# Attention and two expert layers in one kernel: the plan of the order gets other numbers for transfers, and the slots of the work between the matmuls are set again

## The chip, the core and the metric

The kernel runs on one core of one Trainium2 chip. The metric is device time in microseconds (us) of one execution; the kernel before was timed in three runs. TensorE is called PE, its weight loads PEld, VectorE DVE, ScalarE ACT, GpSimd POOL, SyncE SP.

## The reference

```python
# attention: 8 batches x 8 heads x 576 rows x 64; keys and values pooled by 8 to 72
k_p = k.reshape(B, H, 72, 8, D).mean(axis=3)
v_p = v.reshape(B, H, 72, 8, D).mean(axis=3)
scores = matmul(q, k_p^T) / sqrt(D)
attn = exp(scores - max); attn = attn / (sum(attn) + 1e-09)
x = matmul(attn, v_p)                       # becomes 4608 tokens x 512
# first layer, 512 -> 2048 -> 512
h = x @ moe_w_in;  x = maximum(0.01 * h, h) @ moe_w_out
# second layer, 512 -> 2048 -> 512
h = x @ moe2_w_in; out = (h * clip(h + 3, 0, 6) / 6) @ moe2_w_out
```

## The kernel before

**The work.** All matmuls of the two layers keep fp32 accuracy: each operand is split into a high and a low part (fp32r), and three products are added. The attention is cut into 24 units (three for each of the 8 batches). A unit has a load of its queries (tile `q`, one buffer, so the next unit's queries can be fetched only when the scores of the unit before have read it), loads of keys and values (tile `raw`, two buffers), sums over 8 on DVE, scores on PE (L492), a maximum on DVE (L508), exps on ACT (L517), a reciprocal, two normalizations on DVE (L535, L548), transposes on PE (L594, L574), copies of them on ACT, and the values' matmuls on PE (L626). The first layer goes over tiles of 512 tokens: for 16 blocks `f` of 128 hidden units a `gemm1` (12 matmuls, L752 to L754) into a bank `h`, the leaky relu on ACT (L767) and DVE, and a `gemm2` (12 matmuls, L801 to L803). The weights of that layer come in a packed form, 1 MB for each `f`, and are decoded by ACT (L666, L668) and DVE (L671, L679, L322). The first tile uses only the first 8 blocks, and its other half is done later. Later tiles of the first layer go in pairs with 7 products in place of 8 (`Pair1`), and the whole second layer does so too (`Pair`); their left factors are written to DRAM (`left1`, `left2`) and read back.

**What sets the order.** No order is written out by hand. Each piece of work is a task with an engine, a cost in ns and the tasks that it needs. `Plan.place` lays the tasks out in time: one free time for each engine, one of them for all DMAs together; a task that needs another starts no sooner than that one's end plus a lag from a table `LAG` (with `plan.landing` on top behind a DMA). `Plan.order` does this 12 times, forward and back, keeps the shortest result, and issues all instructions in the order of their planned starts; each engine then goes through its own instructions strictly in that order. A DMA costs its bytes divided by a rate, plus a constant. Up to the first `gemm2`, a gap of PE in the plan is filled with small matmuls on zeros (`idle<-zeros`, L1615), one for each 56 ns of the gap beyond 200 ns.

**Which tasks stand where before the plan.** PE's tasks keep the order in which the program lists them. A list of steps (`gemm1`, `gemm2` of one `f`) has numbered slots, and the table `C` says in which slot the scores, transposes, values of a unit, the decoding of a weight block or the making of a left factor are listed: `when0` for the weights in the first tile, `att0` for units 2 to 5 there, `quick` and `slow` for the distances between scores, transposes, the third transpose, values and the next unit's sums; `when1`, `att1`, `att2` and so on for later tiles. `flex` is the number of tasks for which a copy may go to ACT or DVE, whichever the plan finds free.

**Transfers.** All DMAs are issued by SP in one order. A load into a tile is issued when the readers of that tile's former content are done; whatever stands behind it on SP waits as well. A write waits for the instruction that makes its data.

Of the kernel before, what the change touches and what calls it, by code (L numbers as in the profile page):

```python
# [30 lines left out]
C = dict(  # L31
    n32=1,
    soon={0: 2000, 1: 4000, 2: 6000},
    flex=536,
    mid=8,
    half0=3,
    steps0='rffrfffr',
    when0=[0, 0, 0, 4, 3, 5, 13],
    att0=[0, 9, 27, 30],
    sec0=4,  # L40
    half1=0,
    steps1='ffffffffffffffff',
    when1=[9, 14, 15, 19],
    att1=[32, 41],
    sec1=23,
    att2=[7],
    quick=[0, 1, 0, 2, 5],
    slow=[0, 4, 5, 5, 4],
    left1=[[(0, 41), (1, 10)], [(2, 4), (3, 3)]],
    att3=[0, 5, 8, 10, 20, 36],  # L50
    gaps3=[0, 2, 2, 2, 0],
    prep3=[17, 48],
    att5=[11, 19, 33, 44, 54, 62],
    gaps5=[0, 3, 2, 9, 4],
    prep5=[94, 156],
    att7=[0, 19, 35],
    gaps7=[1, 12, 11, 13, 18],
    prep7=[87, 97],
    left2=[[(0, 10)], [(1, 16)], [(2, 22)], [(3, 55), (4, 22), (5, 50)], [(6, 18), (7, 51)]],
)  # L60
SCORES = 1700
EXPS = 1782
TRANSPOSES = 260
FIRST_LOADS = 1.25
WARM_FROM = 2700
ENGINES = ("pe", "act", "dve", "gp", "dma")
FIRST = {"dma": 1700.0, "gp": 600.0, "dve": 700.0}


def _f32(bits):  # L70
# [3 lines left out]
class Buf:  # L74


    def __init__(self, plan, pool, tag, shape, dtype, bufs):
        row = plan.tags.setdefault(tag, [])
        self.prev = row[-bufs] if len(row) >= bufs else None
        if self.prev is not None:  # L80
            self.prev.gone = True
        self.gone = False
        row.append(self)
        self.args = (pool, tag, shape, dtype, bufs)
        self.name = f"{tag}_{len(row)}"
        self.tile = None
        self.users, self.writers, self.readers = set(), {}, {}
# [24 lines left out]
class Plan:  # L112
# [8 lines left out]
        ("dve", "dve"): 125,  # L121
        ("act", "act"): 0,
        ("pe", "pe"): 0,
        ("dma", "dma"): 2150,
    }

    def __init__(self):
        self.tags, self.tasks, self.fill_until, self.sooner = {}, [], None, {}
        self.extra, self.landing = [], 0

    def add(self, engine, cost, emit, reads=(), writes=(), other=None):

        n = len(self.tasks)
        after = set()
        over = lambda d, key: (t for k, v in d.items() if all(a == b for a, b in zip(k, key)) for t in v)
        for v in (*reads, *writes):
            assert not v.buf.gone, v.buf.name
            if v.buf.prev is not None:
                after |= v.buf.prev.users
        for v in reads:  # L140
            before = {t for key in v.keys for t in over(v.buf.writers, key)}
            assert before, v.buf.name
            after |= before
        for v in writes:
            for key in v.keys:
                after.update(over(v.buf.writers, key))
                after.update(over(v.buf.readers, key))
        after.discard(n)
        for v in reads:
            for key in v.keys:  # L150
                v.buf.readers.setdefault(key, set()).add(n)
            v.buf.users.add(n)
        for v in writes:
            for key in v.keys:
                v.buf.writers.setdefault(key, set()).add(n)
            v.buf.users.add(n)
        self.tasks.append(([(engine, cost, emit)] + ([other] if other else []), after))
        self.extra.append(self.landing if engine == "dma" else 0)

    def lag(self, a, b):  # L160

        return self.LAG.get((a, b), 1500 if a == "dma" else 1250 if b == "dma" else 180)

    def place(self, ways, after, then, rank, lag, first, back=False):


# [16 lines left out]
        while done < n:  # L183
            best = None
            for e in ENGINES:
                while waiting[e] and waiting[e][0][0] <= free[e]:
                    _, i, k = heapq.heappop(waiting[e])
                    heapq.heappush(ready[e], (rank[i], i, k))
                while ready[e] and way[ready[e][0][1]] is not None:
                    heapq.heappop(ready[e])  # L190
                while waiting[e] and way[waiting[e][0][1]] is not None:
                    heapq.heappop(waiting[e])
                start = free[e] if ready[e] else waiting[e][0][0] if waiting[e] else None
                if start is not None and (best is None or start < best[0]):
                    best = (start, e)
            start, e = best
            free[e] = start
            if not ready[e]:
                continue
            _, i, k = heapq.heappop(ready[e])  # L200
            starts[i], way[i] = start, k
            free[e] = stop = start + ways[i][k][1]
            end = max(end, stop)
            done += 1
            for j in then[i]:
                left[j] -= 1
                late = self.extra[j if back else i]
                for m, w in enumerate(ways[j]):
                    since[j][m] = max(since[j][m], stop + lag(e, w[0]) + late)
                if not left[j]:  # L210
                    offer(j)
        return starts, way, end

    def order(self):
# [19 lines left out]
        for _ in range(ROUNDS):  # L234
            starts, way, end = self.place(ways, after, then, rank, self.lag, FIRST)
            chosen = [w[k] for w, k in zip(ways, way)]
# [20 lines left out]
def attention_moe_moe(ctx: ExitStack, tc: tile.TileContext, qt, kt, vm, vr, wt, wq, eye, mask, out):  # L257
# [15 lines left out]
    plan = Plan()  # L273
    add = plan.add
# [26 lines left out]
        add("pe", n, emit, reads, writes)  # L301

    def on_dma(nbytes, emit, reads, writes):
        add("dma", nbytes / 340 + 60, emit, reads, writes)

    def other(*way):
        return way if len(plan.tasks) < C["flex"] else None
# [19 lines left out]
    def load(dst, src, nbytes):  # L327

        on_dma(nbytes * (FIRST_LOADS if len(plan.tasks) < 60 else 1), lambda: DMA.dma_start(out=dst.ap(), in_=src), [], [dst])

# [317 lines left out]
    left1 = []  # L648
# [4 lines left out]
    def load_w(f, raw):  # L653
        on_dma(
            1 << 20, lambda: DMA.dma_start(out=raw.get().bitcast(I32), in_=wt[ORDER[f]].bitcast(I32)), [], [raw()]
        )
# [29 lines left out]
    def decode_w(f, raw, t, l):  # L686

        decode(raw, t, l)
        wf = buf(f"w{f}", [128, 4, 512], F32R)
        w[f] = wf  # L690
        hi = wf("hi", lambda t: t[:, 0:2].rearrange("p a n -> p (a n)"))
        lo = wf("lo", lambda t: t[:, 2:4].rearrange("p a n -> p (a n)"))
        copy(hi, t, 1024)
        subtract(lo, t, hi, 1024)
        d = chunk[f]()
        on_dma(1 << 19, lambda: DMA.dma_start(out=d.ap(), in_=t.ap()), [t], [d])
        keep(f, wf)
# [222 lines left out]
    left2 = Left(2)  # L920
# [489 lines left out]
    for u in units[:3]:  # L1410
        g = u.n % 2
        a = a13 if g else a12
# [11 lines left out]
    load(mask_sb, mask, 1536)  # L1424
    fetch(u1)
    add("dve", 70, lambda: DVE.memset(three.ap(), 3.0), [], [three])
    room = {0: 8, 1: 9, 2: 10, 3: 14, 4: 15, 5: 14, 6: 15, 7: 14}
    temps = {}

    def weights(f):  # L1430
# [152 lines left out]
    pairs = [Pair(2 * sum(widths[:i]), n) for i, n in enumerate(widths)]  # L1583
# [20 lines left out]
        for k in range(2):  # L1604
            p.jobs.at(56 + 8 * (3 + 2 * k), lambda nxt=nxt, k=k: nxt.prepare(k))
    for p in [*pairs1, *pairs]:
        plan.landing = 250 if p in pairs else 1300
        if p in pairs:
            p.new_spare()
        p.first()  # L1610
        p.second(p is pairs[-1])
# [66 lines left out]
```

## Time and profile before

| what | value |
|---|---|
| time, median of three runs (lowest to highest) | 1571.47 us (1571.19 to 1572.18) |
| the profiled execution: its time | 1572.92 us |
| the profiled execution: span of the instructions | 1571.1 us |
| PE busy | 1564.6 us, 100% of the span |
| DVE busy | 1157.2 us, 74% |
| ACT busy | 969.7 us, 62% |
| granted clock of PE, mean | 1.00 |
| DMA, mean over the span | 259 GB/s |

The profiled execution took 1.45 us more than the median of the three runs, and 1.8 us lie outside the span of its instructions. A busy PE is one that has instructions in work, the small matmuls on zeros among them; it says nothing on whether that work is needed. The rows on which the prediction rests stand in a section below.

### The profile page before, as it was taken

Reading aid. Unit: us, or ns where it says so; the run is one execution under the profiler, and the core shown is the slowest. Engines: PE = TensorE matmul, PEld = TensorE weight load, DVE = VectorE, ACT = ScalarE, POOL = GpSimd, SP = SyncE. Lnnn points to the kernel's source line nnn. Section 1 sums busy time; section 2 is a strip of 40 time slices with the busy share of each in tenths; the row PEclk is TensorE's granted clock in tenths of the full one; section 3 lists DMA queues with packets and bytes.
Section 4 is the critical chain, followed back from the end, with each engine's and each line's share of the span. In section 5 each row is a group of like instructions: output and inputs, shape, how many; then the busy total and the mean of one; then the engine's idle time right before and its main releaser. Section 6 shows DMA issues by size and latency. Waiting matters only on the chain.

```text
span 1571.1 us, 22819 instructions
## 1 busy us (share of the span) xinstructions
PE 1564.6 (100%) x7971; PEld 1342.9 (85%) x7971; DVE 1157.2 (74%) x2000; ACT 969.7 (62%) x2219; POOL 1.9 (0%) x11
## 2 busy tenths in 40 slices
PE   9999999999999999999999999999999999999999
PEld 8888888888888888888888888898899888889988
DVE  7998568568789776985696579559756856875494
ACT  7886476667877677666655455446545544654454
POOL 0000000000000000000000000000000000000000
PEclk9999999999999999999999999999999999999999
DMA  8899778668896898979976567756866675676564
GB/s 313 298 338 313 256 246 272 211 240 285 286 309 225 294 340 298 325 266 335 320 271 224 200 228 248 254 210 218 291 213 230 236 254 210 228 245 229 210 231 143
DMA packets 128322, 406.32 MB, mean 259 GB/s; under 512 B 18512, under 2 KB 47312, under 8 KB 106448
## 3 DMA queue, kind: packets, MB, share of 16 engines
q1 hardware_dynamic: 128208, 404.87, 74.5%
q8 instruction: 63, 1.03, 0.3%
q14 instruction: 51, 0.42, 0.1%
HBM read 317.79 MB, written 87.03 MB: 258 GB/s over the span
## 4 chain that ended last, share of the span: by engine, by line
PE 95%; DVE 3%; ACT 1%; DMA 1%; issue 0%; SPq 0%; DVEq 0%
PE y L1056 37%; PE h L1056 21%; PE a L1056 12%; PE h L752 3%; PE y L801 3%; PE y L802 3%; PE y L803 3%; PE h L754 3%; PE h L753 3%; PE a L626 2%; PE a L492 2%; DVE w L923 1%; PE a L574 1%; PE idle L1615 1%; PE a L594 1%; DVE gl L1251 0%
## 5 line engine op out<-in xcount | busy, mean ns | idle before, releaser
L923 DVE TENSOR_TENSOR w<-y,w 128x512 f32<-128x512 f32 (+2 forms) x108 | 71.0, 658 | 117.5 <-PE y L1056 115.8
L315 ACT ACTIVATE gh<-w 128x460 fp32r<-128x460 f32 (+1 forms) x140 | 82.2, 589 | 65.2 <-PE y L1056 24.8
L923 DVE TENSOR_TENSOR w<-w 128x460 f32<-128x460 f32 (+2 forms) x168 | 104.9, 645 | 3.4 <-ACT w L767 3.0
L1251 DVE SCALAR_TENSOR_TENSOR gl<-w,gh 128x460 fp32r<-128x460 f32 (+1 forms) x140 | 88.4, 633 | 23.5 <-ACT gh L315 23.2
L1056 PE MATMUL y<-w,xh 128*128 128x512 f32 (+2 forms) x444 | 103.9, 383 | 0.0
L1056 PEld LDWEIGHTS y<-w,xh 128*128 128x128 f32 x444 | 82.6, 188 | 13.0
L312 ACT CAST gh<-w 128x512 fp32r<-128x512 f32 x96 | 59.6, 623 | 41.4 <-PE y L1056 21.5
L1222 ACT ACTIVATE gh<-w,three 128x460 f32<-128x460 f32 (+1 forms) x60 | 40.9, 682 | 71.0 <-DVE w L923 71.0
L1056 PE MATMUL y<-w,raw 128*128 128x460 f32 (+1 forms) x384 | 83.4, 370 | 0.0
L801 PE MATMUL y<-gh,w 128*128 128x512 f32 (+2 forms) x204 | 80.3, 394 | 0.1
L752 PE MATMUL h<-xh,w 128*128 128x512 f32 (+2 forms) x204 | 79.8, 391 | 0.0
L1056 PEld LDWEIGHTS y<-w,raw 128*128 128x128 f32 x384 | 72.1, 188 | 8.2
L802 PE MATMUL y<-gl,w 128*128 128x512 f32 (+2 forms) x204 | 78.3, 384 | 0.0
L803 PE MATMUL y<-gh,w 128*128 128x512 f32 (+2 forms) x204 | 78.2, 383 | 0.0
L753 PE MATMUL h<-xl,w 128*128 128x512 f32 (+2 forms) x204 | 77.9, 382 | 0.0
L754 PE MATMUL h<-xh,w 128*128 128x512 f32 (+2 forms) x204 | 77.9, 382 | 0.0
L1056 PE MATMUL y<-w,xl 128*128 128x512 f32 (+2 forms) x324 | 76.8, 385 | 0.0
L322 DVE TENSOR_TENSOR gl<-w,gh 128x512 fp32r<-128x512 f32 x96 | 65.6, 684 | 12.4 <-ACT gh L312 12.4
L322 DVE TENSOR_TENSOR st<-raw,st 128x512 fp32r<-128x512 f32 x88 | 59.7, 685 | 14.7 <-ACT st L312 14.6
L1056 PE MATMUL y<-gh,raw 128*128 128x462 f32 (+1 forms) x224 | 70.0, 373 | 0.0
L517 ACT ACTIVATE s<-a,mx 128x72 f32<-128x72 f32 x204 | 62.5, 345 | 11.7 <-DVE mx L508 11.7
L1056 PEld LDWEIGHTS y<-w,xl 128*128 128x128 f32 x324 | 60.4, 188 | 10.4
(267 smaller groups left out, 4145.0 us busy)
## 6 DMA issues: line engine op xcount, KB each, us to landing
raw<-left SPq DMA_DIRECT2D x68, 1024.0 KB, 4.8
left<-st SPq DMA_DIRECT2D x176, 256.0 KB, 4.7
xh<-left SPq DMA_DIRECT2D x37, 1024.0 KB, 4.8
xl<-left SPq DMA_DIRECT2D x68, 512.0 KB, 5.1
xh<-left SPq DMA_DIRECT2D x56, 512.0 KB, 5.3
w<-left SPq DMA_DIRECT2D x56, 512.0 KB, 5.2
xl<-left SPq DMA_DIRECT2D x25, 1024.0 KB, 4.9
w<-wt SPq DMA_DIRECT2D x16, 1024.0 KB, 8.2
```

The source lines that it names most:

```text
L315: a = lambda: ACT.mul(out=dst.ap(), in_=src.ap(), mul=scale)
L322: lambda: DVE.tensor_tensor(out=dst.ap(), in0=a.ap(), in1=f32(b.ap()), op=ALU.subtract),
L517: ACT.activation(out=at()[:, c, h, :], in_=s4()[:, c, pi, :], func=AF.Exp, bias=mx.get()[:, c, h : h + 1], accum_out=sm.get()[:, 4 * c + h ...
L752: PE.matmul(out=o, lhsT=hi, rhs=xh.get()[:, k, c0:c1], start=k == 0, stop=False)
L753: PE.matmul(out=o, lhsT=hi, rhs=xl.get()[:, k, c0:c1], start=False, stop=False)
L754: PE.matmul(out=o, lhsT=lo, rhs=xh.get()[:, k, c0:c1], start=False, stop=k == 3)
L801: PE.matmul(out=y[:, n0:n1], lhsT=hi, rhs=gh.get()[:, n0:n1], start=start, stop=False)
L802: PE.matmul(out=y[:, c0:c1], lhsT=hi, rhs=gl.get()[:, c0:c1], start=False, stop=False)
L803: PE.matmul(out=y[:, c0:c1], lhsT=lo, rhs=gh.get()[:, c0:c1], start=False, stop=stop)
L923: on_dve(n, lambda: DVE.tensor_tensor(out=dst.ap(), in0=a.ap(), in1=b.ap(), op=op), [a, b], [dst])
L1056: PE.matmul(out=o, lhsT=l, rhs=r, start=first and i == m == 0, stop=last and i == len(left) - 1 and m == 2, skip_group_check=True,)
L1251: lambda: DVE.scalar_tensor_tensor(out=lo.ap(), in0=v.ap(), scalar=1.0 / 6.0, in1=f32(hi.ap()), op0=ALU.mult, op1=ALU.subtract),
```

## The change

The computation stays as it is, and the instructions are the same but for 30 fewer matmuls on zeros (173 in place of 203) and a few copies that go to another engine. What changes is numbers of two kinds. The plan's reckoning of a DMA: up to the end of the tiles that go one by one it takes bytes / 420 + 40 ns (before bytes / 340 + 60) and a lag of 2100 ns to the reader (before 1500), for `Pair1` a rate of 340 and 900 ns on top of the lag (before 1300), for `Pair` a rate of 400 and nothing on top (before 250); the first loads are no longer stretched by 1.25, and DMA is free from 800 ns on (before 1700). And the slots in `C` are others.

```diff
-    flex=536,
+    flex=540,
-    when0=[0, 0, 0, 4, 3, 5, 13],
-    att0=[0, 9, 27, 30],
+    when0=[0, 0, 5, 3, 10, 6, 12],
+    att0=[0, 9, 26, 28],
-    when1=[9, 14, 15, 19],
-    att1=[32, 41],
-    sec1=23,
+    when1=[8, 15, 21, 23],
+    att1=[36, 57],
+    sec1=37,
-    quick=[0, 1, 0, 2, 5],
+    quick=[0, 2, 1, 2, 8],
...
-FIRST_LOADS = 1.25
+FIRST_LOADS = 1.0
-FIRST = {"dma": 1700.0, "gp": 600.0, "dve": 700.0}
+FIRST = {"dma": 800.0, "gp": 600.0, "dve": 700.0}
...
-        ("dma", "dma"): 2150,
+        ("dma", "dma"): 2500,
...
-        self.extra, self.landing = [], 0
+        self.extra, self.landing, self.rate = [], 0, 420
...
-        return self.LAG.get((a, b), 1500 if a == "dma" else 1250 if b == "dma" else 180)
+        return self.LAG.get((a, b), 2100 if a == "dma" else 1250 if b == "dma" else 180)
...
-        add("dma", nbytes / 340 + 60, emit, reads, writes)
+        add("dma", nbytes / plan.rate + 40, emit, reads, writes)
...
-        plan.landing = 250 if p in pairs else 1300
+        plan.landing, plan.rate = (0, 400) if p in pairs else (900, 340)
```

Three places of the order follow. In the rows a name like `w8_2_543` is the second use of buffer `w8`; the last number counts tiles.

DVE, in the first 20 us, from the sum over the keys of unit 1 (`w15_1`, in two halves) and the maxima of unit 0 (`mx_1`, from the scores in `a_1`, `a_2`) on; before:

```order
L389 TENSOR_REDUCE w15_1_95<-w15_1_95 128x72
L508 TENSOR_REDUCE mx_1_189<-a_1_172 128x6
L389 TENSOR_REDUCE w15_1_95<-w15_1_95 128x72
L508 TENSOR_REDUCE mx_1_189<-a_2_174 128x6
L316 TENSOR_SCALAR keys1_1_191<-w15_1_95 128x72
L508 TENSOR_REDUCE mx_2_275<-y2_1_244 128x6
L528 TENSOR_SCALAR inv_1_277<-sm_1_197 128x12
L508 TENSOR_REDUCE mx_2_275<-y3_1_246 128x6
```

and in the changed kernel:

```order
L389 TENSOR_REDUCE w15_1_91<-w15_1_91 128x72 x2
L508 TENSOR_REDUCE mx_1_169<-a_1_146 128x6
L508 TENSOR_REDUCE mx_1_169<-a_2_148 128x6
L508 TENSOR_REDUCE mx_2_220<-y2_1_186 128x6
L508 TENSOR_REDUCE mx_2_220<-y3_1_188 128x6
L457 TENSOR_TENSOR raw_2_162<-h_1_211,mask_1_172 96x256
L313 CAST vrm0_1_247<-raw_2_162 96x256
L528 TENSOR_SCALAR inv_1_249<-sm_1_202 128x12
```

The second half of unit 1's keys is now summed ahead of the first maximum and no longer between the two, and the sums of unit 0's values (`raw_2`, `vrm0`) stand ahead of `inv_1`, with which the normalization of unit 0 begins. On PE 45 matmuls on zeros stand ahead of unit 0's scores in place of 73, 10 between the scores of units 0 and 1 in place of 35, and 47 ahead of the first `gemm1` in place of 35.

ACT, between the first `gemm1` and the copies of the transposes of unit 2 (`a_16`, `a_17` into `w12_1`, which the values' matmuls of unit 2 read); before:

```order
L312 CAST tr_3_678<-a_15_663 96x384
L312 COPY w12_1_70<-a_16_668 128x384
L668 ACTIVATE w13_1_74<-w15_2_603 128x1024
L312 COPY w12_1_70<-a_17_689 128x384
L312 CAST vbd00_1_78<-raw_4_597 64x2x64
L315 ACTIVATE x32_1_383<-a_18_693 128x2x128
L312 CAST xh_1_385<-x32_1_383 128x128 x2
L666 ACTIVATE w12_1_70<-w15_2_603 128x1024
```

and in the changed kernel:

```order
L666 ACTIVATE w12_1_70<-w10_1_299 128x1024
L767 ACTIVATE u_1_564<-h_3_524 128x384
L312 CAST gh_1_78<-u_1_564 128x384
L312 CAST rem_3_573<-rn_3_567 128x3x32 x2
L666 ACTIVATE w11_1_344<-w14_2_351 128x1024
L312 CAST tr_3_590<-a_15_586 96x384
L668 ACTIVATE st_1_593<-w8_2_543 128x512
L312 COPY w12_1_70<-a_16_602 128x384
L312 COPY w12_1_70<-a_17_608 128x384
```

A piece of the decoding of `w8_2` (L668, into `st_1`), one of the weights for the second tile, now stands ahead of the two copies. On PE the transposes and values of unit 2 have moved as well: they stand behind the second `gemm1` (`h_4`) and ahead of the first `gemm2` (L801), with 7, 7 and 6 matmuls on zeros between them; before, 14 of these and then the first `gemm2` and the third `gemm1` stood there, and the transposes and values came after.

SP, around the load of the queries of unit 4 (`q_4`); before, with the loads of `w8_2`, `w9_2` and `w10_2` behind it:

```order
L887 DMA xr_1_977<-spill_1_705 512x1x64
L329 DMA raw_7_982<-kt 128x1152
L329 DMA q_4_1009<-qt 128x768
L655 DMA w8_2_1015<-wt 128x2048
L655 DMA w9_2_1045<-wt 128x2048
L329 DMA q_5_1096<-qt 128x768
L655 DMA w10_2_1108<-wt 128x2048
```

In the changed kernel `w8_2` and `w9_2` stand 20 and 19 rows ahead of `q_4`,

```order
L329 DMA raw_4_472<-vr 96x512
L329 DMA raw_4_472<-vm 128x1024
L655 DMA w8_2_543<-wt 128x2048
L655 DMA w9_2_570<-wt 128x2048
L329 DMA raw_5_606<-kt 128x1152
L655 DMA w14_3_630<-wt 128x2048
L696 DMA chunk2_1_669<-w12_1_70 128x1024
```

and right ahead of it stand another load of 1 MB and two writes of left factors:

```order
L329 DMA raw_7_887<-kt 128x1152
L655 DMA w15_4_908<-wt 128x2048
L696 DMA chunk5_1_949<-w11_1_344 128x1024
L713 DMA left1_10_1_957<-w0_1_387 128x2x256
L713 DMA left1_10_1_957<-w2_1_627 128x2x256
L329 DMA q_4_971<-qt 128x768
```

`w10_2` is one of the rows between the two pieces. Summed over SP's rows, the transfers up to and with `q_4` carry 20,480 KB in the kernel before and 25,088 KB in the changed one; those up to and with `w8_2` carry 12,609 KB in the changed one.

## Rows read from the trace of the kernel before

**Rows 1.** The page, span and section 1 (busy us, share of the span, instructions).

```profile
span 1571.1 us, 22819 instructions
PE 1564.6 (100%) x7971; PEld 1342.9 (85%) x7971; DVE 1157.2 (74%) x2000; ACT 969.7 (62%) x2219; POOL 1.9 (0%) x11
```

**Rows 2.** The chain that ended last, 0 to 60 us, in order: start, us, what.

```profile
0.99 6.91 PE idle L1615 x73
7.90 1.54 PE a L492 x24
...
10.06 3.74 ACT s L517 x24
...
30.56 2.06 PE idle L1615 x35
32.62 0.23 PE h L752
36.88 0.81 PE idle L1615 x14
37.83 0.47 PE y L801
```

**Rows 3.** Stretches of 40 us: busy us of each engine, granted clock, DMA share, GB/s.

```profile
0.00:40.00 40.00, 38.03 (x413) 34.85 (x414) 30.92 (x60) 29.40 (x104) 1.91 (x11) 1.00 0.87 310
...
80.00:120.00 40.00, 40.00 (x223) 33.92 (x222) 38.43 (x71) 33.26 (x81) 0.00 (x0) 1.00 0.96 343
120.00:160.00 40.00, 40.00 (x175) 32.48 (x174) 35.12 (x58) 26.98 (x56) 0.00 (x0) 1.00 0.91 304
400.00:440.00 40.00, 39.52 (x231) 32.68 (x230) 31.66 (x56) 31.87 (x102) 0.00 (x0) 1.00 0.91 321
1360.00:1400.00 40.00, 39.42 (x187) 34.56 (x186) 35.88 (x66) 22.83 (x42) 0.00 (x0) 1.00 0.71 245
```

**Rows 4.** Timeline of DVE, 7 to 11 us: start, us, instruction, idle before.

```profile
7.70 0.75 DVE L389 TENSOR_REDUCE w<-w 128x72 f32<-128x576 f32 x1 [2.17 <-DMA w<-kt]
9.42 0.61 DVE L508 TENSOR_REDUCE mx<-a 128x6 f32<-128x432 f32 x1 [0.97 <-PE a L492]
9.95 0.74 DVE L389 TENSOR_REDUCE w<-w 128x72 f32<-128x576 f32 x1
```

**Rows 5.** Timeline of DVE, 33 to 40 us.

```profile
33.59 1.21 DVE L322 TENSOR_TENSOR w<-w,w 128x1024 fp32r<-128x1024 f32 x1
...
35.93 1.34 DVE L389 TENSOR_REDUCE raw<-raw 128x144 f32<-128x1152 f32 x1
...
39.20 0.95 DVE L548 TENSOR_TENSOR s<-s,inv 128x768 f32<-128x768 f32 x1
```

**Rows 6.** Timeline of ACT, 30 to 43 us.

```profile
30.62 1.14 ACT L666 ACTIVATE w<-w 128x1024 f32<-128x1024 f32 x1
31.66 0.31 ACT L517 ACTIVATE s<-a,mx 128x72 f32<-128x72 f32 x1
...
35.22 0.56 ACT L767 ACTIVATE u<-h 128x384 f32<-128x384 f32 x1
...
42.76 0.49 ACT L312 COPY w<-a 128x384 f32<-128x384 f32 x1
```

**Rows 7.** Timeline of PE, the transposes of unit 2.

```profile
42.05 0.49 PE L574 MATMUL a<-ident,s 128*128 128x128 f32 x3
```

**Rows 8.** DMA, 0 to 75 us: GB/s in 40 slices of 1.875 us, and the total.

```profile
GB/s 11 306 237 342 345 340 417 284 346 415 415 290 15 212 289 434 389 305 414 387 385 112 350 411 66 44 267 249 411 418 419 387 371 278 326 325 341 431 424 149
DMA packets 6133, 23.16 MB, mean 309 GB/s; under 512 B 1263, under 2 KB 1391, under 8 KB 4719
```

**Rows 9.** Issue of q_4 on SP.

```profile
66.06 0.33 SPq L329 DMA_DIRECT2D q<-qt  x1
```

**Rows 10.** Instructions of tile q, 45 to 75 us: its three loads, landing times.

```profile
DMA to landing us min/median/max: 3.4/5.1/8.8
```

**Rows 11.** Timeline of PE, 70 to 74 us: the scores that read q_4.

```profile
73.04 1.11 PE L492 MATMUL a<-keys,q 64*128 64x72 f32 x16
```

More of the change, by code (lines that the diff above doesn't have):

```diff
@@ L42 @@
     steps1='ffffffffffffffff',
-    when1=[9, 14, 15, 19],
-    att1=[32, 41],
-    sec1=23,
-    att2=[7],
-    quick=[0, 1, 0, 2, 5],
[L48 to L52, printed above, removed]
-    att5=[11, 19, 33, 44, 54, 62],
[L54 to L59, printed above, removed]
+    when1=[8, 15, 21, 23],
+    att1=[36, 57],
+    sec1=37,
+    att2=[9],
+    quick=[0, 2, 1, 2, 8],
+    slow=[0, 4, 5, 5, 8],
+    left1=[[(0, 60), (1, 7)], [(2, 7), (3, 7)]],
+    att3=[0, 4, 8, 10, 22, 37],
+    gaps3=[0, 0, 1, 2, 0],
+    prep3=[22, 57],
+    att5=[11, 19, 33, 44, 54, 62],
+    gaps5=[0, 4, 1, 9, 1],
+    prep5=[99, 163],
+    att7=[0, 17, 35],
+    gaps7=[1, 11, 12, 12, 2],
+    prep7=[80, 80],
+    left2=[[(0, 10)], [(1, 22)], [(2, 17)], [(3, 60), (4, 21), (5, 45)], [(6, 15), (7, 56)]],
 )
@@ L1426, in attention_moe_moe @@
     add("dve", 70, lambda: DVE.memset(three.ap(), 3.0), [], [three])
-    room = {0: 8, 1: 9, 2: 10, 3: 14, 4: 15, 5: 14, 6: 15, 7: 14}
+    room = {0: 8, 1: 9, 2: 10, 3: 14, 4: 15, 5: 14, 6: 15, 7: 14, 8: 15, 9: 14}
     temps = {}
```

## Prediction

> **What bounds the kernel now.** I read the page's busy times first: PE works in 1564.6 of 1571.1 us [rows 1], so the kernel is a chain of matmuls and only 6.5 us of the span have no matmul at all. More time hides in matmuls on zeros, and the chain of the first 60 us shows where: 73 of them ahead of unit 0's scores (6.91 us), 35 ahead of the first `gemm1` (2.06 us), 14 between the second `gemm1` and the first `gemm2` (0.95 us from 36.88 to 37.83) [rows 2]. The stretches say the same from the other side: PE is full from 80 to 160 us and misses 0.48 us at 400 to 440 and 0.58 us at 1360 to 1400 [rows 3]. A change of order can therefore win a few us at the start and about 1.1 us later; it can lose wherever PE comes to wait for something that it doesn't wait for now. The second limit in the first 160 us is DMA: its engines are 0.87 to 0.96 busy there, and the most that a stretch of 40 us moved is 343 GB/s, at a share of 0.96 [rows 3]. The plan before reckoned with 340, so its order asked for about what the transfers give. The plan now reckons with 420 in this part.
>
> **The change, part by part.** The sum goes against the profiled execution, 1572.92 us; the median of the runs is 1.45 us less.
>
> *The start.* With 45 matmuls on zeros in place of 73, unit 0's scores can begin about 1 us sooner than at 7.90. But the first maximum on DVE now stands behind both sums over unit 1's keys. The first of these waited for its load until 7.70, and one takes 0.74 to 0.75 us [rows 4]: two in a row end at about 9.2, where the maximum began at 9.42 before. So the exps come 0.2 to 0.3 us sooner than at 10.06 [rows 2], not 1 us. Behind them the sums of unit 0's values stand ahead of `inv_1`, two instructions of some 0.35 us each by my estimate (a 1024-element pass takes 1.21 [rows 5], and these have 256 elements and a fixed part), which gives it back. The other uncertainty is the clock. The first 73 matmuls on zeros took 95 ns each, the 35 later ones 59 ns [rows 2]; so most of the first ran at 1.2 GHz and the later ones at 2.4. With fewer of them the scores (1.54 us) may run at the lower level, up to 1.5 us more. I take **+0.2, from -0.3 to +1.5**.
>
> *Unit 2 and the first `gemm2`.* In the new order PE does the transposes and values of unit 2 between the second `gemm1` and the first `gemm2`. That work is only moved; what costs is the waiting inside it. I follow ACT and DVE from the first `gemm1`, left at 32.6 [rows 2]. Before, three subtractions stood ahead of unit 2's maxima; now they stand behind, so that the 12 exps (3.56 us from 31.66 to 35.22 [rows 6]) end at about 34.7. DVE then has the sum over unit 3's keys (1.27), `inv_3`, a short sum of unit 3's values (half of the former, some 0.6), the reciprocal, `rn_3`, a decoding pass of 1024 (1.14 from start to start) and the rest of the weights, and brings the third transpose's source at about 37.4 [rows 5]. ACT has in that time a decoding pass (1.04 from start to start), the relu and its cast, the casts of the weights' rest, another decoding pass, the copy `tr_3`, and is at 38.6 [rows 6]. There stands the new row, L668 of `w8_2`: half of a pass, 0.5. Then the two copies, 0.37 each (0.49 less the overlap), and PE's values can start at 39.9. PE has been through with `h_4` since 36.9 [rows 2]; of the 3.0 us between, 0.8 is transposes (three of 0.49 less overlap [rows 7]). So 2.2 us are empty or zeros, where 0.95 were: **+1.2**, if `w8_2` has landed by 38.6. It stands behind 12,609 KB, 12.91 MB. At the 310 GB/s of the first 40 us they are through at 41.6; at 343, at 37.6. The middle, 39.6, makes ACT wait 1.0, with PE's values and, behind them on PE, the first `gemm2` and all the rest. I take **+2.2, from +1.0 to +4.2**.
>
> *The queries of unit 4.* Before, `q_4` was issued at 66.06 [rows 9] and landed 5.1 us later (the median of the three loads [rows 10]), at 71.16; the scores read it at 73.04 [rows 11], with 1.9 us to spare. Now 25,088 KB, 25.69 MB, are ahead of its landing instead of 20,480. In the first 75 us 23.16 MB went through at a mean of 309 GB/s, and hardly anything in the first 1.9 us [rows 8]. At 343 GB/s the 25.69 MB take 74.9 us; with the empty head they are through at 76.8. The scores are wanted at 73.04, less about 1.75 us because unit 4 now stands one step sooner in the list (a `gemm1` of 384 columns is 12 matmuls of 0.18 us, 24 of them from 32.62 to 36.88 [rows 2]), plus the 2.4 us lost above: 73.7. The wait is 1.2 to 3.1 us, and I take the middle. If more than 343 is reached it is nothing (the best slices show 410 to 434 [rows 8]); half way between 343 and 309, 326, it is 5.0. So **+2.1, from 0 to +5.0**. The scores hold the step behind them on PE, and with it the banks that ACT and DVE wait for.
>
> *The loads behind it.* Up to 160 us the traffic stays dense (0.96, then 0.91 [rows 3]), and each load of 1 MB takes 3.06 us at 343 where the plan gives it 2.50 at 420. Four in a row are 2.2 us late. Against this stand the larger lag, 2100 for 1500, which asks for a lone 1 MB load at the same time as before (2.50 + 0.04 + 2.10 against 3.08 + 0.06 + 1.50, both 4.64), and the share of 0.91, which leaves some room. I take **+0.8, from 0 to +2.2**.
>
> *All that comes later.* For `Pair1` a load of 1 MB is asked for 0.18 us sooner than before (3.08 + 0.04 + 2.10 + 0.90 against 5.94), for `Pair` 0.13 us later (4.76 against 4.89); that is small beside the room at a share of 0.71 [rows 3]. The slots are all new, however, and with them the chances of single waits. The best is that the two holes of 0.48 and 0.58 close; the worst that I count is one load of 1 MB that is late in full, 3.1. I take **+0.4, from -1.1 to +3.1**. The 30 matmuls on zeros that are gone are in the terms above, since they stood where PE waited.
>
> The sum: 0.2 + 2.2 + 2.1 + 0.8 + 0.4 = **+5.7 us**, 1578.6 for a profiled execution and **1577.2** for the median. The bounds add up to -0.4 and +16.0: 1571.1 and 1587.5.
>
> **A rule that speaks for the change.** In the rows the transfers of the first 75 us run at 309 GB/s in the mean, and in single slices at up to 434 [rows 8]. The Trainium skill, page "DMA: Bandwidth & Descriptors", section "Anatomy of one DMA — SWDGE (gpsimd) path", fits a transfer (there one that GpSimd issues) as 2.0 us plus its bytes at 436 GB/s, which is nearly the plan's new pair of numbers. By it, as an estimate, `q_4` would land at 61 us if nothing else held it, and the term would be nothing. The trace agrees in its best slices only; no stretch of 40 us comes near.
>
> **The rivals.** *The transfers keep up.* SP issued its loads in bursts before because it waited for decoded weights between them (slices of 15 to 112 GB/s at 23, 40 and 46 us [rows 8]); the new order has these writes later, and the holes may fill. Then `w8_2` and `q_4` are there in time: +0.2 + 1.2, less up to 1.1 for the two later holes, 1571.8 to 1572.9; I say 1572.3, no change. Against it: at 80 to 120 us there were no holes, and the rate was 343 [rows 3].
>
> *Faster.* One mechanism: the start comes sooner, because the scores begin 1 us earlier and the loads land as the plan now says. It needs the second half of unit 1's keys by 7.7 and `w8_2` by 37. Then 1.0 us at the scores and the 1.7 us of the 30 matmuls on zeros (0.059 each [rows 2]) are gained, with the two later holes 3.8: 1567.7. For it: the zeros are on the chain. Against it: the row of 7.70 [rows 4]. It decides from about 9.0 for the first maximum on.
>
> *Congestion that feeds itself.* If the transfers go on at 309 GB/s, `q_4` is through at 83.1, 9.4 us late. With 0.2 + 2.2 + 0.8 + 0.4 that makes +13.0, 1584.5. For it: 309 is what was measured; against it: this mean holds the bursts' holes.
>
> **How the numbers follow.** A measurement of this kernel can tell about 0.2%, 3.1 us, from no change: faster is below 1568.3, slower above 1574.6. The forecast has a chance of 0.55, with a range of its own from 1574 to 1582; transfers that keep up 0.22; faster 0.12; congestion 0.11. Slower is 0.51 of the forecast's 0.55 and the congestion, 0.62; the same is 0.22 and the rest of the forecast, 0.26; faster 0.12. The range goes from 1568.5, which leaves out most of the faster case, to 1584, which leaves out most of the congestion.
>
> **What would show it.** In the changed kernel's waits PE should have some 1 to 3 us in front of unit 2's values, released by ACT's copies, with ACT held before L668 of `w8_2` by a DMA at 38 to 41 us; a wait of 1 to 4 us at the scores of unit 4, released by the load of `q_4`, near 75; the first exps near 9.8; DMA at a share above 0.9 from 20 us on. The prediction is wrong if the stretch from 0 to 80 shows 340 GB/s or more and none of these waits, or if the first `gemm2` comes before 38 us.

## The result, and the profile after

The changed kernel takes 1585.74 us in the median of six runs (1578.09 to 1587.30), against 1571.33 for the kernel before in runs beside it: a ratio of 1.0082, interval 1.0060 to 1.0104. By the medians it is slower by 14.4 us; ratios and intervals, here and below, go by the means (1584.2 against 1571.3). The forecast said slower, 1577.2, with a range up to 1584; the time lies above the range.

The six runs are not alike, and they go, but for small differences, with the mean granted clock:

| run | us | mean clock of PE |
|---|---|---|
| 1 | 1578.09 | 0.999 |
| 2 (profiled) | 1581.31 | 0.998 |
| 3 | 1585.61 | 0.995 |
| 4 | 1585.87 | 0.995 |
| 5 | 1586.87 | 0.996 |
| 6 | 1587.30 | 0.995 |

The profiled execution is one of the faster ones, so the trace below holds +8.4 us of span (1571.1 to 1579.5) and not +14.4. The page's first lines of the changed kernel:

```profile
span 1579.5 us, 22792 instructions
PE 1565.8 (99%) x7941; PEld 1342.4 (85%) x7941; DVE 1157.5 (73%) x2002; ACT 970.8 (61%) x2217; POOL 1.9 (0%) x11
```

PE is busy for 1.2 us more than before and its span is 8.4 us longer, so this time PE stands empty for most of the difference [rows 1]. The stretches of the changed kernel show where; the columns are those of [rows 3]:

```profile
0.00:40.00 40.00, 34.48 (x348) 32.06 (x349) 26.55 (x54) 27.02 (x100) 1.91 (x11) 0.91 0.88 322
40.00:80.00 40.00, 37.92 (x280) 33.09 (x280) 38.09 (x67) 34.28 (x99) 0.00 (x0) 1.00 0.97 360
80.00:120.00 40.00, 40.00 (x230) 34.31 (x229) 36.31 (x68) 26.81 (x71) 0.00 (x0) 1.00 1.03 360
400.00:440.00 40.00, 40.00 (x236) 33.03 (x235) 32.51 (x57) 30.99 (x87) 0.00 (x0) 1.00 0.89 302
1360.00:1400.00 40.00, 40.00 (x193) 35.97 (x192) 38.62 (x70) 24.61 (x44) 0.00 (x0) 1.00 0.66 230
```

Up to 40 us PE's clock is 0.91 and 5.5 us are empty (2.0 before [rows 3]), to 80 us another 2.1. From 80 to 160 us PE is full, and the two holes at 400 and 1360 us have closed (40.00 each, against 39.52 and 39.42 in [rows 3]). DMA moved 360 GB/s from 40 to 120 us, more than the 343 that I had taken for its best.

The first 24 us in shorter stretches, changed kernel:

```profile
8.00:12.00 4.00, 2.89 (x46) 2.60 (x44) 2.75 (x5) 2.43 (x15) 0.00 (x0) 1.00 1.09 313
12.00:16.00 4.00, 4.00 (x27) 4.00 (x26) 0.83 (x2) 3.66 (x25) 0.00 (x0) 0.57 1.01 373
16.00:20.00 4.00, 2.00 (x23) 1.90 (x22) 3.10 (x9) 1.43 (x9) 0.00 (x0) 0.92 1.02 420
20.00:24.00 4.00, 4.00 (x25) 4.00 (x25) 2.73 (x9) 2.14 (x8) 0.00 (x0) 0.66 0.76 313
```

The clock is at 0.57 of full from 12 to 16 us, that is mostly at 1.2 GHz, and again at 0.66 from 20 to 24. The timeline of PE in the changed kernel shows what came before:

```profile
0.98 4.90 PE L1615 MATMUL idle<-zeros 128*128 128x128 bf16 x45 [0.98 <-DVE three L1426]
6.81 1.56 PE L492 MATMUL a<-keys,q 64*128 64x72 f32 x24 [0.92 <-DMA q<-qt]
8.31 0.73 PE L1615 MATMUL idle<-zeros 128*128 128x128 bf16 x10
10.15 1.56 PE L492 MATMUL y<-keys,w 64*128 64x72 f32 x24 [1.11 <-DMA w<-qt]
11.64 5.03 PE L413 MATMUL h<-raw,ident 96*96 96x64 f32 x32
...
20.00 1.51 PE L574 MATMUL a<-ident,s 128*128 128x128 f32 x6 [2.00 <-DVE s L548]
...
36.44 0.42 PE L752 MATMUL h<-xh,w 128*128 128x384 f32 x1
```

The 45 zeros end at 5.9, and PE stands empty for 0.92 until `q` lands. The 10 zeros end at 9.0, and it stands empty for 1.11 until unit 1's queries land. Then the sums of the values (L413) take 5.03 us where they took 3.41 in the kernel before, which has

```profile
12.87 3.41 PE L413 MATMUL h<-raw,ident 96*96 96x64 f32 x32
```

At 18 us PE is empty for 2.00, waiting for DVE's L548, the normalization of unit 0. On DVE of the changed kernel:

```profile
16.71 0.42 DVE L457 TENSOR_TENSOR raw<-h,mask 96x256 f32<-96x256 f32 x1 [3.87 <-PE h L413]
...
17.37 0.16 DVE L528 TENSOR_SCALAR inv<-sm 128x12 f32<-128x12 f32 x1
...
18.89 0.96 DVE L548 TENSOR_TENSOR s<-s,inv 128x768 f32<-128x768 f32 x1
```

and on DVE of the kernel before:

```profile
13.84 0.17 DVE L528 TENSOR_SCALAR inv<-sm 128x12 f32<-128x12 f32 x1 [0.26 <-ACT s L517]
...
14.98 0.96 DVE L548 TENSOR_TENSOR s<-s,inv 128x768 f32<-128x768 f32 x1
...
17.96 0.41 DVE L457 TENSOR_TENSOR raw<-h,mask 96x256 f32<-96x256 f32 x1
```

Before, `inv_1` and L548 came at 13.84 and 14.98, and the product L457, which waits for PE's sums, at 17.96. Now L457 stands ahead, DVE waits 3.87 us in front of it for those sums, and L548 comes at 18.89. The first `gemm1` starts at 36.44 (above), where the kernel before has

```profile
32.43 0.42 PE L752 MATMUL h<-xh,w 128*128 128x384 f32 x1
```

That is +4.0 us. The first `gemm1` of the second tile, behind which nothing is lost up to 160 us, stands in the kernel before and in the changed one at

```profile
99.37 0.51 PE L752 MATMUL h<-xh,w 128*128 128x512 f32 x1
```

```profile
106.45 0.51 PE L752 MATMUL h<-xh,w 128*128 128x512 f32 x1
```

That is +7.1. The remaining 1.3 us to the +8.4 of the span are lost later. PE's waits of the changed kernel, over the whole span, name the same places at the start:

```profile
PE a L574 <- DVE s L548: 3.0, 2, 2.0
PE y L492 <- DMA w<-qt: 1.1, 1, 1.1
...
PE a L492 <- DMA q<-qt: 0.9, 1, 0.9
```

### The profile page after: what moved, and what is told of

Its sections match the earlier page's. It is cut to its first block, busy times and chain, and to the rows that moved or that the text cites. A ratio compares the mean times of both kernels' runs of the same rounds, so it can differ in the third digit from the quotient of the medians.

```text
span 1579.5 us, 22792 instructions
## 1 busy us (share of the span) xinstructions
PE 1565.8 (99%) x7941; PEld 1342.4 (85%) x7941; DVE 1157.5 (73%) x2002; ACT 970.8 (61%) x2217; POOL 1.9 (0%) x11
## 3 DMA queue, kind: packets, MB, share of 16 engines
q8 instruction: 63, 1.03, 0.3%
## 4 chain that ended last, share of the span: by engine, by line
PE 86%; DVE 9%; DMA 4%; ACT 1%; issue 1%; SPq 0%; DVEq 0%; ACTq 0%
PE y L1056 33%; PE h L1056 22%; PE a L1056 11%; PE y L801 3%; PE y L802 3%; PE y L803 3%; DVE w L923 2%; PE h L752 2%; PE h L754 2%; PE h L753 2%; PE a L626 2%; PE a L492 2%; DMA x<-x 1%; PE a L574 1%; DVE gl L1251 1%; DVE gl L322 1%
## 5 line engine op out<-in xcount | busy, mean ns | idle before, releaser
L312 ACT CAST gh<-w 128x512 fp32r<-128x512 f32 x96 | 59.9, 624 | 41.0 <-PE y L1056 23.7
L801 PE MATMUL y<-gh,w 128*128 128x512 f32 (+2 forms) x204 | 80.7, 396 | 0.0
L752 PE MATMUL h<-xh,w 128*128 128x512 f32 (+2 forms) x204 | 79.2, 388 | 0.0
L753 PE MATMUL h<-xl,w 128*128 128x512 f32 (+2 forms) x204 | 77.9, 382 | 0.0
L754 PE MATMUL h<-xh,w 128*128 128x512 f32 (+2 forms) x204 | 77.9, 382 | 0.0
L1056 PE MATMUL y<-w,xl 128*128 128x512 f32 (+2 forms) x324 | 76.8, 385 | 0.0
```

Source lines behind the costliest of these rows:

```text
L752: PE.matmul(out=o, lhsT=hi, rhs=xh.get()[:, k, c0:c1], start=k == 0, stop=False)
L753: PE.matmul(out=o, lhsT=hi, rhs=xl.get()[:, k, c0:c1], start=False, stop=False)
L754: PE.matmul(out=o, lhsT=lo, rhs=xh.get()[:, k, c0:c1], start=False, stop=k == 3)
L801: PE.matmul(out=y[:, n0:n1], lhsT=hi, rhs=gh.get()[:, n0:n1], start=start, stop=False)
L1056: PE.matmul(out=o, lhsT=l, rhs=r, start=first and i == m == 0, stop=last and i == len(left) - 1 and m == 2, skip_group_check=True,)
```

## The experiments

Each was timed beside the kernel before, whose median in the five groups was 1571.1 to 1571.8. "Zeros" are the matmuls on zeros.

| run | us (lowest to highest) | ratio, interval |
|---|---|---|
| changed, zeros back (73, 35) | 1580.69 (1577.62 to 1581.97) | 1.0056, 1.0044 to 1.0068 |
| the same, 36 more at the third gap | 1576.87 (1575.84 to 1578.85) | 1.0040, 1.0028 to 1.0053 |
| before, fewer zeros (45, 10) | 1574.41 (1571.49 to 1579.88) | 1.0020, 1.0011 to 1.0029 |
| new reckoning, slots of before | 1586.21 (1582.07 to 1587.24) | 1.0089, 1.0076 to 1.0102 |
| new slots, reckoning of before | 1575.35 (1574.42 to 1576.94) | 1.0028, 1.0017 to 1.0038 |
| changed, head restored | 1585.63 (1584.54 to 1588.18) | 1.0095, 1.0081 to 1.0109 |
| changed, rate and lag restored | 1571.82 (1570.18 to 1576.84) | 1.0011, 1.0002 to 1.0020 |
| the same, with 73 and 35 zeros | 1572.12 (1570.54 to 1574.56) | 1.0004, 0.9995 to 1.0013 |
| before, pairs' reckoning alone new | 1578.42 (1577.03 to 1579.13) | 1.0045, 1.0033 to 1.0058 |
| changed, lag alone new (rate 340) | 1573.72 (1572.81 to 1576.16) | 1.0017, 1.0008 to 1.0025 |
| changed, rate alone new (lag 1500) | 1594.54 (1591.74 to 1596.36) | 1.0142, 1.0127 to 1.0158 |
| head restored, `q_4` ahead | 1586.43 (1584.06 to 1587.45) | 1.0094, 1.0080 to 1.0109 |
| changed, rate 300 | 1573.03 (1572.14 to 1574.83) | 1.0010, 1.0002 to 1.0019 |
| changed, rate 380 | 1576.30 (1574.79 to 1578.71) | 1.0033, 1.0021 to 1.0044 |
| changed, `flex` 480 (rate 420) | 1584.04 (1579.90 to 1587.54) | 1.0082, 1.0069 to 1.0095 |
| the same, rate 340 | 1577.06 (1574.27 to 1577.69) | 1.0032, 1.0020 to 1.0044 |

**What the clock costs.** The plan's order stays, only zeros are added.

```diff
-                out += [self.fill] * int((self.starts[i] - busy - 200) / 56)
+                out += [self.fill] * (int((self.starts[i] - busy - 200) / 56) + next(more, 0))
```

with `more = iter([28, 25])`:

> The changed kernel with its order kept, and 28 more matmuls on zeros ahead of unit 0's scores (73 as before) and 25 more between the scores of units 0 and 1 (35 as before). Theory (clock): with 45 and 10 of them PE stands empty at 5.9 to 6.8 and 9.0 to 10.2 us, its clock falls, and the work up to 24 us runs partly at 1.2 GHz; with the zeros back the granted clock of 8 to 24 us is 1.00, the first gemm1 starts at 33 to 34 us in place of 36.4, and the time is 1574 to 1579, 6 to 12 us under the changed kernel's 1585.7. Rival (transfers): the loss is from late loads, which zeros don't touch: 1583 to 1588.

It came out at 1580.69, with clocks of 0.998 to 1.000: 5.1 us back, and 9.6 left. Neither theory alone. Its trace still has the 2.0 us in front of L574, and a clock of 0.85 and 0.73 in the two stretches of 4 us from 16 to 24 us. So the same with `iter([28, 25, 0, 0, 0, 36])`, which puts zeros into that gap:

> The changed kernel with 73 and 35 zeros, as in the run with the zeros back, and 36 more between the sums of unit 1's values and the transposes of unit 0, where PE stood empty for 2.0 us from 17.9 on. Theory (clock): the clock stays at 1.00 from 8 to 24 us, and 1 to 3 us come back from 1580.7: 1577 to 1580. Rival (what is left of the loss is the order, not the clock): 1580 to 1582.

1576.87, all five runs at 1.000, some 3 us apart at most. Stretches and PE's timeline of this run (its lines are numbered one higher):

```profile
12.00:16.00 4.00, 4.00 (x46) 3.93 (x45) 1.22 (x3) 3.19 (x22) 0.00 (x0) 1.00 0.99 400
16.00:20.00 4.00, 3.96 (x57) 3.72 (x55) 3.79 (x12) 2.24 (x15) 0.00 (x0) 1.00 1.03 425
```

```profile
17.03 2.12 PE L1616 MATMUL idle<-zeros 128*128 128x128 bf16 x35
19.20 0.84 PE L575 MATMUL a<-ident,s 128*128 128x128 f32 x6
...
34.43 0.42 PE L753 MATMUL h<-xh,w 128*128 128x384 f32 x1
```

The transposes of unit 0 still come 3.1 us later than before (19.20; before at 16.12), since DVE's order is the changed one, but at full clock, and the first `gemm1` is at 34.43: 2.0 us of the 4.0 were the order, 2.0 the clock. Over the medians, zeros in the three gaps give back 1585.74 - 1576.87 = 8.9 us, with the order as it was; I put these to the clock, and 5.5 are left. The two profiled executions are 2.6 us apart (spans of 1579.5 and 1576.9), so most of the 8.9 isn't in these traces; it lies in the slower executions of the changed kernel, of which there is no trace.

The reverse, on the kernel before with `iter([-28, -25])`:

> The kernel before with its order kept, and 45 and 10 matmuls on zeros at the two places in place of 73 and 35. Theory (clock): the same fall of the clock without any of the change: mean clock 0.995 to 0.999, 1576 to 1587. Rival (transfers): 1570 to 1573, since no transfer moves.

1574.41, less than the theory asked for, with 0.995 to 0.999 in the eleven runs. The stretches of this run:

```profile
8.00:12.00 4.00, 3.08 (x40) 2.86 (x39) 2.41 (x5) 2.89 (x19) 0.00 (x0) 0.69 1.06 353
12.00:16.00 4.00, 4.00 (x29) 3.87 (x28) 2.78 (x8) 3.31 (x23) 0.00 (x0) 0.50 1.07 338
16.00:20.00 4.00, 4.00 (x21) 4.00 (x21) 0.62 (x3) 3.76 (x14) 0.00 (x0) 0.53 0.98 395
```

So taking zeros out lowers the clock without any of the change, and costs 3.3 us. That is less than in the changed kernel, although the clock lies low for 12 us here; the changed kernel's order opens more gaps on PE, but that this makes the difference was not tried.

**Which half, and which number.** The kernel with the new reckoning and `C` as before:

> The plan's new reckoning of transfers with the slots of before. Theory (clock): the new reckoning sets the zeros (45 and 10 again), so this half carries the loss: 1578 to 1588 with a clock below 1. Rival (slots): the new slots carry it, 1570 to 1575.

1586.21, as the whole change. The clock doesn't account for each single run: the longest of this kernel took 1587.24 at 0.999. With `C` as changed and the numbers of the reckoning as before:

> The new slots with the reckoning of before (73 and 35 zeros). Theory (clock): clock 1.00 up to 24 us, 1570 to 1577. Rival (slots): 1578 or more, with the waits of the changed kernel at unit 2's and unit 4's work.

1575.35 at a clock of 1.000: the slots cost some 4 us by themselves. The reckoning has a head and a rate. The head:

```diff
-FIRST_LOADS = 1.0
+FIRST_LOADS = 1.25
-FIRST = {"dma": 800.0, "gp": 600.0, "dve": 700.0}
+FIRST = {"dma": 1700.0, "gp": 600.0, "dve": 700.0}
```

> The changed kernel with the two numbers for the head of the plan as before (DMA free from 1700 ns, first loads stretched by 1.25); rates, lags and slots as changed. The plan then sets 70 and 20 zeros ahead of the first two scores. Theory (the head's two numbers set too few zeros and the clock falls): clock 1.00 up to 12 us, 1575 to 1581. Rival (the rate of 420 and the lag of 2100 order the loads badly): 1582 to 1588.

1585.63; my theory of the head falls. Its clock is 1.00 up to 24 us, and it loses as much later. The chain of this run around the scores of unit 4, and a stretch:

```profile
68.98 9.51 DMA q<-qt
78.49 0.14 issue
78.62 3.17 PE a L492 x32
```

```profile
78.00:84.00 6.00, 5.38 (x37) 4.65 (x38) 5.32 (x11) 5.43 (x25) 0.00 (x0) 0.54 0.90 285
```

`q_4` takes 9.51 us from issue to landing; PE's waits put 3.5 us to it, and behind that the clock falls to 0.54 and the scores take 3.17 us. Next rate and lag, with `C` and the head as changed:

```diff
-        self.extra, self.landing, self.rate = [], 0, 420
+        self.extra, self.landing, self.rate = [], 0, 340
-        return self.LAG.get((a, b), 2100 if a == "dma" else 1250 if b == "dma" else 180)
+        return self.LAG.get((a, b), 1500 if a == "dma" else 1250 if b == "dma" else 180)
-        add("dma", nbytes / plan.rate + 40, emit, reads, writes)
+        add("dma", nbytes / plan.rate + 60, emit, reads, writes)
-        plan.landing, plan.rate = (0, 400) if p in pairs else (900, 340)
+        plan.landing, plan.rate = (600, 400) if p in pairs else (1500, 340)
```

(with `("dma", "dma")` at 2150 again):

> The changed kernel with the rate of 340, 60 ns and the lag of 1500 restored up to the pairs (for the pairs the sum of lag and landing stays as changed); the head's two numbers and the slots as changed, 44 and 20 zeros. Theory (head): the clock still falls, 1577 to 1585. Rival (rate and lag): 1572 to 1577 in spite of the few zeros.

1571.82: nearly all of the loss is gone, although only 44 and 20 zeros stand at the start and the clock falls in seven of the eleven runs (0.995 to 1.000). The rival is right. The lag and the rate apart; the lag alone new is the changed kernel with rate 340 and 60 ns:

> The changed kernel with the rate of 340 and 60 ns per load restored up to the pairs, but the lag of 2100 kept, and the rest as changed (54 and 20 zeros). Theory 1 (the rate of 420 does the harm, since the transfers don't reach it): 1571 to 1576. Theory 2 (the lag of 2100 does the harm: it lets DVE put other work ahead of the normalizations and moves loads forward): 1578 to 1587.

and the rate alone new has the lag lines of the last diff without the rate's:

> The changed kernel with the lag of 1500 restored up to the pairs, but the rate of 420 and 40 ns kept, and the rest as changed (35 and 10 zeros). Theory 1 (rate): 1578 to 1588, with PE waiting for loads of queries between 45 and 90 us. Theory 2 (lag): 1571 to 1577, with a clock below 1 from the few zeros.

1573.72 and 1594.54. It is the rate. Without the larger lag the kernel is 9 us slower still, above the range of either theory; this run also has the fewest zeros (35 and 10) and the lowest clock (0.991 to 0.997), so whether the lag shields from the rate or the zeros make the difference stays open. In it PE waits for loads of queries for 4.6 us in two places, 1.5 ahead of unit 0's scores and 3.1 later:

```profile
PE a L492 <- DMA q<-qt: 4.6, 2, 3.1
```

Then the run with rate and lag restored, with `iter([29, 15])`:

> The run with rate and lag restored, with 73 and 35 zeros in place of 44 and 20. Theory (what spread its times from 1570.2 to 1576.8 is the clock): all runs at a clock of 1.00, within 2 us of one another, at 1570 to 1572. Rival (the spread is in the transfers): the spread stays.

1572.12 at 1.000 in all eleven runs. The spread fell from 6.7 to 4.0 us, not to 2, and the median didn't move; this kernel can't be told from the one before.

**Does any new list cost as much?** The kernel before with only the pairs' numbers changed (the lag and rate up to the pairs as before):

```diff
-        plan.landing = 250 if p in pairs else 1300
+        plan.landing, plan.rate = (600, 400) if p in pairs else (1500, 340)
```

> The kernel before with its slots and its reckoning up to the pairs, and the changed reckoning for the pairs alone (rate 340 with 3000 ns behind a DMA for the first layer's pairs, rate 400 with 2100 for the second layer's). Theory: the pairs' part is worth nothing that can be measured, 1569 to 1573. Rival (a part of the loss is there): 1574 or more.

1578.42, a surprise: 7 us lost. The chain of this run:

```profile
291.70 7.98 DMA raw<-wq
...
300.85 0.37 ACT tr L312
301.27 2.61 PE a L626 x13
```

A load of weights that took 7.98 us ends late at 299.7, ahead of the pairs (their first matmul is at 360 us), so at a place that these numbers don't speak of; I take it that a new number anywhere makes the plan's 12 rounds end in another list. So new lists cost by themselves, and the rate had to be told from that. With the changed kernel's rate stepped, `self.rate` at 300 and at 380:

> The changed kernel with a rate of 300 in place of 420 up to the pairs. Theory (the rate is the cause): the transfers give more than is asked, 1571 to 1577. Rival (any new list costs, whatever the rate): 1571 to 1586, in no order with the rate.

> The changed kernel with a rate of 380 in place of 420 up to the pairs. Theory (rate): between the 1573.7 of a rate of 340 and the 1585.7 of 420, 1575 to 1583, with some wait for a load before 130 us. Rival (any new list costs): no order with the rate.

and with another list, `flex` at 480, at both rates:

> The changed kernel with flex at 480 in place of 540, which gives other engines to some copies and other orders to all that follow, at the rate of 420. Theory (rate): 1582 to 1592 again. Rival (list): anywhere from 1571 to 1590.

> The same flex of 480 with the rate at 340. Theory (rate): 1571 to 1578, 8 us or more under the same list setting at 420. Rival (list): not told apart from it.

The times go with the rate: 1573.0 at 300, 1573.7 at 340 (lag alone new), 1576.3 at 380, 1585.7 at 420; and 1577.1 and 1584.0 with the other list. The list is worth a few us, the last step of the rate, from 380 to 420, 9.4; with the other list 340 and 420 are 7.0 apart, less than the 8 of the theory. What tells the rate from the list best is all runs together: the six at a rate of 420 and with the zeros that the plan sets took 1584.0 to 1594.5, the seven others of the table with a rate of 300 to 380 and the zeros of the plan 1571.8 to 1578.4. But the 1576.9 of the changed list with its three gaps filled, at a rate of 420, lies among the latter. So at a full clock the rate of 420 isn't told apart from another list; its harm is seen with the gaps on PE that it leaves and the low clock that follows them, and the mean clock goes with the rate as well (0.995 to 0.999 at 420 in the changed kernel, 0.999 to 1.000 at 380, 1.000 at 300).

**What gives way.** In the run with the head restored, `q_4` waits behind a load and three writes. The edit puts those behind it, in the list that `order` gives out (`moved` holds the load of `w15_4` and the writes to `left1` that stood between it and `q_4`):

```diff
+        todo = [i for i in todo[: q + 1] if i not in moved] + moved + todo[q + 1 :]
```

> The kernel of the run with the head restored (rate 420 and lag 2100, 1585.6 us, 3.5 us of PE waiting for the load of q_4, 6.7 us lost around it), with one edit: the load of w15_4 and three writes of left factors, 1.75 MB that stood right ahead of q_4 on SP, stand right behind it; no other engine's order moves. Theory (traffic that the plan takes to be through by then holds up q_4): the wait falls below 1 us and 4 to 6 us come back, 1579 to 1582. Rival (the wait is not of these four transfers, or goes over to the decoding of w15_4): 1584 to 1588.

1586.43. The wait for `q_4` is gone, as the theory says, and nothing is won, as the rival says. PE's largest wait of this run, the chain that leads to it, and the stretch (L759, L774 and L319 are L752, L767 and L312 of the listing):

```profile
PE h L759 <- ACT u L774: 3.9, 1, 3.9
```

```profile
107.68 3.87 DMA left<-st
111.65 0.62 ACT st L319
112.81 0.50 PE h L759
```

```profile
104.00:112.00 8.00, 4.93 (x22) 3.74 (x20) 3.78 (x6) 1.36 (x4) 0.00 (x0) 1.00 1.10 374
```

A write of a left factor landed at 111.6, ACT waited for the tile that it reads (`st`, three buffers), the relu behind that on ACT came late, and PE stood for 3.9 us, while DMA moved 374 GB/s. Behind it the clock falls to 0.69 from 112 to 116 us. Up to the first `gemm1` of the second tile the move had won 4.9 us (it starts at 103.17, against 108.08 in the run with the head restored). There PE met this write; in the run with the head restored ACT waits for it too, until 112.3, but PE is late itself and doesn't stand. The run with the new reckoning and the slots of before, where nothing was moved, has the same wait, of 2.9 us. So the move uncovered this wait and didn't make it. That the plan asks for more bytes by then than are moved is my reading of it; no run tests it at this place.

## Why the prediction was wrong, step by step

**What bounds it: right in kind.** The forecast said that a rate of 420 asks for more than the transfers give, and that PE would come to wait for it. The runs with the rate at 300 to 420 show that it costs, and the runs with the rate alone new and with the head restored show PE waiting for queries (3.1 and 3.5 us); what the forecast left out is that most of the price comes by the clock. My ceiling of 343 GB/s was too low: from 20 to 80 us the changed kernel moved 349 GB/s (the kernel before 301), and the run with `flex` at 480 and the rate of 420 moved 385 from 40 to 80 us:

```profile
DMA packets 5136, 20.92 MB, mean 349 GB/s; under 512 B 1022, under 2 KB 1534, under 8 KB 3654
```

```profile
40.00:80.00 40.00, 39.21 (x291) 34.96 (x290) 38.91 (x71) 36.13 (x105) 0.00 (x0) 1.00 1.00 385
```

Both are still below 420. The Trainium skill, page "DMA: Bandwidth & Descriptors", section "Specifications", gives some 358 GB/s as the limit of the memory for one core. The best stretch of 40 us in the changed kernel, 360, lies near it, but the 385 of the other run lie above it, so it wasn't a ceiling here.

**The start, +0.2 with a bound of +1.5: the step that failed.** In the profiled execution it is +4.0 at the first `gemm1`, 2.0 of it by the order and 2.0 by the clock; more of the clock's share lies in the other executions. Two sentences of it were wrong. "Two instructions of some 0.35 us each" were costed by their length; the first of them waits for sums on PE, and so `inv_1`, which stands behind it, waits too (3.87 us). And of the clock I priced only unit 0's scores, 1.5 us at the lower level. The clock fell after the gaps, not in the first scores: these still took 1.56 us. It took the values' sums and the transposes with it, and fell again behind the third gap. I named "fewer zeros" as a gain in time on PE and did not ask what stands there in their place: gaps of 0.92 and 1.11 us, because `q` and unit 1's queries land only at 6.8 and 10.1. The first exps came at 10.10, and not the 0.2 to 0.3 us sooner than 10.06 that I had worked out.

**Unit 2 and the first `gemm2`, +2.2: too high.** The empty time and zeros between `h_4` and L801 came to 2.0 us, near the 2.2 that I had worked out without the load; read in the same way, from start to start, they were 1.1 before, and not 0.95. The wait for `w8_2` didn't come: ACT of the changed kernel has

```profile
42.20 0.48 ACT L312 CAST tr<-a 96x384 fp32r<-96x384 f32 x1
42.58 0.70 ACT L668 ACTIVATE st<-w 128x512 int32<-128x512 uint32 x1
```

with L668 right behind `tr_3`. The load was issued at 34.88 and landed 6.5 us later, at 41.4, near the late end of my 37.6 to 41.6; ACT, which I had at L668 at 38.6, came there at 42.58, 4.0 us late like the start. About +0.9 is left of the term. Losses on one chain cover each other: I had added this wait as if the start were in time.

**`q_4`, +2.1: right in kind, too high.** It was issued at

```profile
70.90 0.35 SPq L329 DMA_DIRECT2D q<-qt  x1
```

and landed 7.0 us later, at 77.9, where I had 76.8. The scores follow at once:

```profile
76.85 0.39 PE L803 MATMUL y<-gh,w 128*128 128x512 f32 x1
78.08 1.64 PE L492 MATMUL a<-keys,q 64*128 64x72 f32 x32 [0.84 <-ACT u L767]
```

PE was empty for 0.84 us before them; the wait is put to the relu there, which ends within 0.2 us of the landing, so this execution doesn't tell the two apart. With the three gaps filled, where PE comes there 2.1 us sooner, the wait for `q_4` is 1.0 us. In the run with the head restored, where the start lost 1.0 us, the same load costs 3.5 us of waiting and the clock behind it. The sum had a slip as well: 12 matmuls of 0.18 us are 2.1 us and not 1.75, with which the term would have been +2.5.

**The loads behind it, +0.8, and what comes later, +0.4:** in the profiled execution no loss from the second tile up to 160 us, then 1.3 us to the end, with the two old holes closed as in the best case.

**The sum.** At a clock held up by zeros the changed kernel is 5.5 us slower, where the forecast of the order and the loads had 5.7, but its terms were made up otherwise (2.0 of it is the start), so that the two agree is luck. The other 8.9 us came back with zeros in the gaps and a clock of 1.000; for the clock I had a bound of 1.5 in one term and nothing in the ones behind. Of the rivals, transfers that keep up and the faster case were wrong; congestion that feeds itself gave 1584.5, the nearest number of all, by a wait of 9.4 us that didn't come, which is luck too.

**Open.** Why one gap on PE is followed by the lower clock and another of its size isn't was not tried: the kernel with rate 380 has 49 and 15 zeros, empty times of 1.23 and 0.60 us in the same places and of 1.5 us from 16 to 20 us, and a clock of 1.00 up to 24 us. The Trainium skill, page "TensorE: Matmul & The Clock Gate", section "Part 1: The HAM clock gate (the "warmup" mystery)", says that the moment at which the clock changes differs from run to run of one kernel; the six runs of the changed kernel, at mean clocks of 0.995 to 0.999, are in keeping with that, but the moment itself is seen in one of them alone. The rows give a clock of 1.00 for the first 8 us too, where the 45 zeros took 109 ns each, against 59 for each of the 35 in the kernel before [rows 2]; for this part the length of the zeros tells more than the row. Nor were the 2.0 us between the two starts at full clock taken apart into DVE's order and the rest.

## What to carry to other kernels

Small matmuls that fill PE's waits can be worth more than the time that they stand for (8.9 us in the changed list, but 3.3 in the list of before and nothing that can be measured in the one with rate and lag restored): before a plan is allowed to drop them, look at when the data for the next real matmul lands, in the trace, and fill up to that. A plan that orders transfers should reckon with a rate that they hold with all the traffic over a long dense stretch, not with that of the best slice or the best 40 us: here 300 and 340 cost 1.6 and 2.0 us, 380 cost 4.9 and 420 cost 14.4. Moving one late transfer ahead uncovered the next one that was late. And where a scheduler lists all the work anew, compare several lists at one setting before a few us are put down to the setting.

## What had not been expected of the hardware

Empty times of 0.92 and 1.11 us on PE within 5 us, with 10 small matmuls and one set of scores between them, were followed by a stretch of 4 us at a clock of 0.57, and one of 2.00 us by one at 0.66; with the gaps filled the clock stayed at 1.00. The six times of the changed kernel spread over 9 us, at mean clocks of 0.995 to 0.999, where the kernel before spread over 2. And DMA moved 360 GB/s over 40 us with its engines busy throughout (a share of 1.03), against 343 at 0.96 in the kernel before; another list at the same rate moved 385 at a share of 1.00.
